# Logits, ranks, rows and lists of every batch moved to PSUM banks T and U; weight conversions due later, their stores issued from GpSimd

## The chip, the cores and the metric

The kernel runs on one core of a Trainium2 chip. The metric is the device time of one execution in microseconds (us); where several executions are timed, the median stands for them. A profiled execution gives the trace, with a time of its own.

## The reference

Three stages follow each other, with 4 batches of 448 tokens, 12 heads of 64 and a model width of 768:

```python
scores = cap * tanh(q @ k.T / sqrt(64) / cap)           # attention, per batch and head
attn = exp(scores - max); attn /= attn.sum + 1e-9
x = concat_heads(attn @ v)                               # 1792 x 768
h = x @ w_in; g = h * clip(h + 3, 0, 6) / 6              # FFN, d_ff = 2048
y = g @ w_out
logits = y @ w_gate; e = argmax(logits)                  # 8 experts, one per token
out = softmax(logits)[e] * sigmoid(y @ w_output_gate)[e] * (relu(y @ w1[e]) @ w2[e])
```

The FFN's weights `w_in` and `w_out` arrive as 64-bit floats, all else as 32-bit floats.

## The kernel before

**Stages.** Attention is done per pair of heads (24 pairs, 6 per batch). For a pair, TensorE transposes q and k, which ScalarE (L495) and VectorE (L499) split into a high and a low part (`qk`); TensorE forms the scores (L527) in the double banks S0 and S1; ScalarE takes tanh (L536) and exp (L540); VectorE sums the exponentials (`es`, L548); TensorE multiplies with v (L558) and sums over rows (L564); the division follows (L591 to L601), and the result stands in `xTa` or `xTb` in two parts. The FFN of a batch has 28 products (16 with a slice of `w_in`, 12 with one of `w_out`), each of three passes (L610 to L612). A product's weights come from DRAM into `wr` (L633, on SP's queue) and are split into `ws` by ScalarE (L636) and VectorE (L639). After a batch's FFN come the routing (`route`: logits L762, their transposes L773, ranks L799 and L800), the token rows (`rows`: transposes L854, eight groups per batch, copied out at L291 or L293) and a listing of tokens (`listing`, L899). After the last batch the experts' slots follow (`ring`, `hTm`, L1423).

**Conversion of the FFN's weights.** `cv` converts the 64-bit weights to 32 bits once, in 56 parts, two per product of the first batch's FFN. A part is loaded on GpSimd's queue (L394) into one of five buffers, scaled by VectorE or ScalarE (L400, L402), put together by three VectorE operations (L405, L408, L411) in one of three `cva` tiles, and stored to DRAM (L416) on SP's queue, whence L633 loads it in each batch.

**Banks.** PSUM has the double banks S0 and S1 and the single ones T, U, F0 and F1. The FFN's products use F0 and F1 in turn. From the second batch on attention uses T (transposes of q and k, row sums) and U (product with v). Routing, rows and listing of batches 0, 1 and 3 take F0 and F1, those of batch 2 take T and U (`TU`).

**Order.** The program is issued by a planner (`Work.run`): each operation has a due time `at`, a length `ns`, what it comes after and the buffers it holds. For each engine the planner takes, of the operations that are ready in its own count of time, the one due first, and issues it. What comes out is a fixed order per engine; on the chip each engine works its list off in that order and waits on semaphores. `conv` parts were due at `i * 4.4e3` for the first 16 (the attention of batch 0 is planned from 0 to `T0` = 70e3) and 30e3 ahead of their product for the others:

```python
at = i * 4.4e3 if i < 16 else max(T0, t_ff(i // 2) - 30e3)
x = work.add("pool", at - 6e3, 1500, load, ...)
stored[i] = work.add("sp", at + 3e3, 500, store, [y], [ha], size=w * 512)
```

Of the kernel before, what the change touches and what calls it, by code (L numbers as in the profile page):

```python
# [68 lines left out]
class Work:  # L69
# [5 lines left out]
    LAG = {"pe": 200, "act": 150, "dve": 130, "pool": 150, "sp": 0}  # L75
    TO_PE = {"act": 160, "dve": 70}
    WINDOW = 10240 / 3
    PRE, POST, RATE = 1400, (1100, 2000), 0.36

    def __init__(self):  # L80
        self.ops = []
# [12 lines left out]
    def run(self):  # L94
# [10 lines left out]
        soon = {e: [] for e in self.LAG}  # L105
        due = {e: [] for e in self.LAG}
        free = dict.fromkeys(self.LAG, 0)
        tick = cols = 0
        line = 0
        slow = 2  # L110
# [13 lines left out]
        while done < len(self.ops):  # L124
# [23 lines left out]
            if e == "pe":  # L148

                x = t  # L150
# [31 lines left out]
def attention_ffn_moe(  # L182
# [15 lines left out]
    nc = tc.nc  # L198
    B, H, S, D = q.shape
# [113 lines left out]
    Sp, Tp, Up, F, U2 = banks("S0", "S1"), banks("T"), banks("U"), banks("F0", "F1"), banks("U", "F1")  # L313
# [25 lines left out]
    work = Work()  # L339
# [3 lines left out]
    T0, T1, TL = 70e3, 174e3, 120e3  # L343
# [14 lines left out]
    def t_ff(i):  # L358
        b, j = divmod(min(i, B * NW - 1), NW)
        if i >= B * NW:  # L360
            return T0 + (B - 1) * T1 + TL + (i - B * NW) * 3e3
        x = cost[j] / cost[-1]
        return T0 + b * T1 + x * (T1 if b < B - 1 else TL)
# [7 lines left out]
    wv_out = w_out_i.rearrange("(t p) (d w) -> p t d w", p=128, w=256)  # L371
    stored, turned_w = {}, {}

    def cv(i):
        key, j = parts[i][:-1], parts[i][-1]
        at = i * 4.4e3 if i < 16 else max(T0, t_ff(i // 2) - 30e3)
        h, ha = F64.take(), CVA.take()
        if key[0] == "i":
            n = KD // 2
            src = wv_in[:, j * n:(j + 1) * n, key[1], :]  # L380
            dst = ws_in[key[1]]
        else:
            n = NH2
            o = key[1] * HF + j * n
            src = wv_out[:, o:o + n, key[2], :]
            dst = ws_out[key[1]][key[2]]
        t = h.t[:, 0:n]
        w = n * 128
        lo = t.rearrange("p t w two -> p (t w) two")[:, :, 0]
        g = t.rearrange("p t w two -> p (t w) two")[:, :, 1]  # L390
        a = ha.t[:, 0:w]

        def load():
            G.dma_start(out=t.rearrange("p t w two -> p t (w two)"), in_=src)  # L394

        def scaled(eng):

            t = g.bitcast(F32)
            if eng == "dve":
                V.tensor_scalar(out=t, in0=t, scalar1=2.0 ** -112, scalar2=None, op0=ALU.mult)  # L400
            else:
                A.activation(out=t, in_=t, func=ACTF.Copy, scale=2.0 ** -112)  # L402

        def b0():
            V.tensor_scalar(out=a, in0=lo, scalar1=29, scalar2=None, op0=ALU.logical_shift_right)  # L405

        def b1():
            V.scalar_tensor_tensor(out=a, in0=g, scalar=3, in1=a, op0=ALU.logical_shift_left, op1=ALU.bitwise_or)  # L408

        def b2():  # L410
            V.scalar_tensor_tensor(  # L411
                out=a, in0=g, scalar=-(1 << 31), in1=a, op0=ALU.bitwise_and, op1=ALU.bitwise_or
            )

        def store():
            nc.sync.dma_start(  # L416
                out=dst[:, j * n:(j + 1) * n], in_=a.rearrange("p (t w) -> p t w", w=128).bitcast(F32)
            )

        x = work.add("pool", at - 6e3, 1500, load, [turned_w.get(i - 3)] if i < 16 else [], [h], size=w * 1180)  # L420
        s = work.add(("dve", "act"), at, (65 + w // 2, 30 + w), scaled, [x], [h])
        y = work.add("dve", at, 65 + w // 2, b0, [x], [h, ha])
        y = work.add("dve", at, 65 + w, b1, [s, y], [h, ha])
        y = turned_w[i] = work.add("dve", at, 65 + w, b2, [y], [h, ha])
        stored[i] = work.add("sp", at + 3e3, 500, store, [y], [ha], size=w * 512)


    NH = B * H
# [321 lines left out]
    def route(b):  # L750

        t0 = t_ff((b + 1) * NW) + 1e3
        soon = t0 + SOON if b == B - 1 else t0 + 2e3
        R = TU if b == B - 2 else F
        hl, hr = R.take(), ROUTE.take()
        ys = [yT[b, d] for d in range(KD)]
        lp = hl.t
# [84 lines left out]
    def rows(b, c, ys, hr, wd):  # L842
# [3 lines left out]
            rowbuf[b] = ROWS.take(), []  # L846
        hw, done = rowbuf[b]
        for half in range(2):
            hp = (TU if b == B - 2 else F).take()

            def trans(half=half, tp=hp.t):
                for j in range(KD // 2):
                    d = half * (KD // 2) + j
                    nc.tensor.transpose(tp[:P, j * 128:(j + 1) * 128], ys[d][0].t[:, c * P:(c + 1) * P], ident)  # L854

            o = c * RW + half * w_rows
            src = hp.t[:P, 0:w_rows]
            x = work.add("pe", t0, 330, trans, [y[1] for y in ys], [hp] + [y[0] for y in ys])
            x = work.add(
                ("act", "dve"), t0 + 1e3, (371, 465), copier(hw.t[:, o:o + w_rows], src), [x], [hp, hw])  # L860
            done.append(x)
# [13 lines left out]
    def listing(b):  # L875
# [6 lines left out]
        for j, h in enumerate((h0, h1)):  # L882
# [8 lines left out]
        done.append(work.add(  # L891
            "dve", t0, 535, lambda: V.tensor_tensor(
                out=m, in0=m, in1=ids.to_broadcast([P, C, PG]), op=ALU.mult), [x], [h2, hr]))
        hp = (TU if b == B - 2 else F).take()
        acc = hp.t[:PG, 0:128]

        def sums():
# [270 lines left out]

    plan = [(t_head(2 * n - 2) - 1 if n else -2, lambda n=n: pair_qk(n)) for n in range(NH // 2)]
    plan += [(t_head(2 * n) if n else -1, lambda n=n: pair(n)) for n in range(NH // 2)]  # L1170
    plan += [(i * 4.4e3 if i < 16 else t_ff(i // 2) - 30e3, lambda i=i: cv(i)) for i in range(len(parts))]
    plan += [(t_ff(i), lambda i=i: step(i)) for i in range(len(ff))]
    plan += [(t_ff(5) + 1, quiet), (t_ff(NW) - 1, zeros)]
    fin = {}
# [377 lines left out]
```

## Time and profile before

| | |
|---|---|
| three runs | 1067.36 us median (1066.06 to 1068.58) |
| the profiled execution | 1065.96 us, span 1064.2 us |
| busy: TensorE, VectorE, ScalarE, GpSimd | 96%, 68%, 62%, 9% of the span |
| DMA | 199.24 MB, 187 GB/s over the span |

The first 85 us are batch 0's attention, with conversions between; then FFN products and the attention of the next batch run side by side until about 600 us, the last FFN until 740 us, and the experts' slots until the end. A busy TensorE is one whose matmuls overlap or follow without a gap; VectorE's and ScalarE's shares are means over stages that differ.

### The profile page before, as it was taken

What the parts mean: (1) busy time and instruction counts of PE and PEld (TensorE: products, weight loads), DVE (VectorE), ACT (ScalarE), POOL (GpSimd) and SP (SyncE); (2) the same over time, 40 slices, a digit from 0 to 9 for tenths busy, and PEclk for the clock granted to TensorE, in tenths of its full rate; (3) what the DMA queues carried; (4) which work ended last, traced back from release to release, by engine and by line L of the source; (5) the groups of instructions that cost most, each with busy time, mean ns of one, the idle gap of its engine ahead of it and who ended that gap; (6) DMA issues with size and microseconds to landing.
All of it is one profiled execution on the core that took longest, in us unless ns stands there. A gap on an engine that the chain in (4) does not pass through costs nothing.

```text
span 1064.2 us, 17020 instructions
## 1 busy us (share of the span) xinstructions
PE 1024.5 (96%) x5764; PEld 799.7 (75%) x5764; DVE 725.5 (68%) x1154; ACT 661.0 (62%) x917; POOL 93.6 (9%) x122
## 2 busy tenths in 40 slices
PE   6879999999999999999999999999899999999996
PEld 4436778876778787678878799998787777887774
DVE  5999988975763664674475482535986767786763
ACT  6987767755654764474575262535576776876763
POOL 3211222110000000000000100000030101111001
PEclk9989999999999999999999999999899999999999
DMA  9789889962242333234222266354358789979464
GB/s 277 234 244 270 260 289 282 292 206 84 69 157 83 100 125 91 84 103 144 83 86 87 64 247 217 122 189 165 112 164 304 260 289 335 316 260 339 142 187 126
DMA packets 113998, 199.24 MB, mean 187 GB/s; under 512 B 43579, under 2 KB 68027, under 8 KB 113345
## 3 DMA queue, kind: packets, MB, share of 16 engines
q1 hardware_dynamic: 104304, 161.90, 47.0%
q0 software_dynamic: 9600, 36.19, 10.6%
q8 instruction: 47, 0.77, 0.3%
q14 instruction: 47, 0.38, 0.1%
HBM read 224.19 MB, written 25.76 MB: 235 GB/s over the span
## 4 chain that ended last, share of the span: by engine, by line
PE 70%; DVE 14%; issue 10%; DMA 3%; ACT 2%; POOL 0%; SPq 0%; POOLq 0%; DVEq 0%; ACTq 0%
PE F L610 12%; PE F L612 11%; PE F L611 11%; PE S L610 6%; PE S L611 6%; PE S L612 6%; PE U L558 5%; PE S L527 5%; PE F L1423 2%; DVE es L548 2%; DMA out_dram<-y,tkd 2%; DVE cva L408 1%; DVE cva L411 1%; DVE ring L1274 1%; DVE ws L639 1%
## 5 line engine op out<-in xcount | busy, mean ns | idle before, releaser
L639 DVE TENSOR_TENSOR ws<-wr,ws 128x768 fp32r<-128x768 f32 (+1 forms) x112 | 119.4, 1067 | 79.5 <-ACT ws L636 76.9
L636 ACT ACTIVATE ws<-wr 128x768 fp32r<-128x768 f32 (+1 forms) x112 | 104.6, 934 | 38.8 <-PE F L611 27.1
L610 PE MATMUL F<-gT,ws 128*128 128x448 f32 x320 | 120.1, 375 | 1.6 <-ACT xTb L293 1.0
L611 PE MATMUL F<-gT,ws 128*128 128x448 f32 x320 | 117.0, 366 | 0.0
L612 PE MATMUL F<-gT,ws 128*128 128x448 f32 x320 | 117.0, 366 | 0.0
L536 ACT ACTIVATE S<-S,rcap 112x896 f32<-112x896 f32 x96 | 91.1, 980 | 20.0 <-PE S L527 19.4
L540 ACT ACTIVATE ee<-S,capt 112x896 f32<-112x896 f32 x96 | 93.5, 1015 | 0.2
L527 PE MATMUL S<-qk 64*112 64x448 f32 x576 | 77.3, 393 | 12.2 <-ACT qk L495 5.2
L610 PE MATMUL S<-ring,hTm 128*128 128x384 f32 x224 | 81.9, 366 | 0.0
L527 PEld LDWEIGHTS S<-qk 64*112 64x112 f32 x576 | 47.5, 176 | 40.8 <-issue 12.7
L611 PE MATMUL S<-ring,hTm 128*128 128x384 f32 x224 | 76.4, 341 | 0.9 <-DVE ring L1274 0.9
L612 PE MATMUL S<-ring,hTm 128*128 128x384 f32 x224 | 76.3, 341 | 0.0
L610 PE MATMUL F<-xTa,ws 128*128 128x448 f32 x192 | 73.7, 384 | 0.8 <-DVE lg L780 0.6
L610 PE MATMUL F<-xTb,ws 128*128 128x448 f32 x192 | 73.6, 383 | 0.9 <-DVE lg L780 0.6
L610 PEld LDWEIGHTS F<-gT,ws 128*128 128x128 f32 x320 | 60.1, 188 | 16.0 <-issue 8.7
L1274 DVE TENSOR_TENSOR ring<-w2B,ring 128x768 fp32r<-128x768 f32 x56 | 52.6, 955 | 28.5 <-ACT ring L1270 26.9
L612 PE MATMUL F<-xTb,ws 128*128 128x448 f32 x192 | 70.2, 366 | 0.0
L611 PE MATMUL F<-xTb,ws 128*128 128x448 f32 x192 | 70.2, 366 | 0.0
L558 PE MATMUL U<-ee,v 112*64 112x448 f32 x336 | 70.0, 556 | 0.0
L612 PE MATMUL F<-xTa,ws 128*128 128x448 f32 x192 | 69.8, 364 | 0.0
L611 PE MATMUL F<-xTa,ws 128*128 128x448 f32 x192 | 69.5, 362 | 0.0
L663 ACT ACTIVATE r<-F,three 128x448 f32<-128x448 f32 x64 | 40.6, 635 | 45.3 <-PE F L612 44.5
(291 smaller groups left out, 2263.8 us busy)
## 6 DMA issues: line engine op xcount, KB each, us to landing
wr<-wsi SPq DMA_DIRECT2D x64, 384.0 KB
wr<-wso SPq DMA_DIRECT2D x48, 512.0 KB
w1A<-in_moe_w_dram SPq DMA_DIRECT2D x42, 512.0 KB
w2A<-in_moe_w_dram SPq DMA_DIRECT2D x56, 384.0 KB
w1B<-in_moe_w_dram SPq DMA_DIRECT2D x42, 512.0 KB
w2B<-in_moe_w_dram SPq DMA_DIRECT2D x56, 384.0 KB
spare<-in_moe_w_dram SPq DMA_DIRECT2D x72, 256.0 KB
spare<-in_moe_w_dram SPq DMA_DIRECT2D x96, 192.0 KB
```

Of the source, the lines that this page charges most:

```text
L527: nc.tensor.matmul(out=h.t[:P, r, 0:S], lhsT=w[o, 1, i, (c0 + c) * P:(c0 + c + 1) * P], rhs=w[o, 0, j], start=(t == 0), stop=(t == 2))
L536: lambda sv=sv: A.activation(out=sv, in_=sv, func=ACTF.Tanh, scale=rcap[:P]), [s] + caps, [h])
L540: lambda sv=sv, he=he: A.activation(out=he.t, in_=sv, func=ACTF.Exp, scale=capt[:P]), [x], [h, he])
L548: lambda he=he, one=one: V.tensor_tensor(out=es, in0=one.t, in1=he.t, op=ALU.add),
L558: nc.tensor.matmul(out=uv[64 * r:64 * r + 64, 0:S], lhsT=by_head(hv)[:, r, c], rhs=et[c][0].t[:, r], start=(c == 0), stop=(c == C - 1))
L610: nc.tensor.matmul(out=acc, lhsT=lh, rhs=rh, start=first, stop=False)
L611: nc.tensor.matmul(out=acc, lhsT=lh, rhs=rl, start=False, stop=False)
L612: nc.tensor.matmul(out=acc, lhsT=ll, rhs=rh, start=False, stop=last)
L636: lambda: A.activation(out=s[:, 0, 0:n], in_=t, func=ACTF.Copy), [x], [hw, hs])
L639: lambda: V.tensor_tensor(out=s[:, 1, 0:n], in0=t, in1=s[:, 0, 0:n].bitcast(F32), op=ALU.subtract),
L663: "act", t1, 518, lambda: A.activation(out=r, in_=acc, func=ACTF.Relu, bias=three), [last], [ha, hr])
L1274: lambda: V.tensor_tensor(out=hs.t[:, 1, 0:w], in0=raw(), in1=hs.t[:, 0, 0:w].bitcast(F32), op=ALU.subtract),
```

## The change

The conversions' due times are set anew: the first 16 are due from `T0 - 16e3` on at steps of 1e3, the others 40e3 ahead of their product. Their stores go from SP's queue to GpSimd's, with the same due time as the load. Batches 0 and 1 use T and U for routing, rows and listing, as batch 2 did (batch 3 keeps F0 and F1). Three of the planner's own numbers change: GpSimd is taken to be free from 2800 ns on, its DMAs to need 4000 instead of 2000 ns after the transfer, and a load's issue to take 800 instead of 1500 ns.

```diff
-    PRE, POST, RATE = 1400, (1100, 2000), 0.36
+    FIRST = 2800
+    PRE, POST, RATE = 1400, (1100, 4000), 0.36
...
+        free["pool"] = self.FIRST
...
+    def conv_at(i):
+        return T0 - 16e3 + i * 1e3 if i < 16 else max(T0, t_ff(i // 2) - 40e3)
+
     def cv(i):
-        at = i * 4.4e3 if i < 16 else max(T0, t_ff(i // 2) - 30e3)
+        at = conv_at(i)
...
         def store():
-            nc.sync.dma_start(
+            G.dma_start(
...
-        x = work.add("pool", at - 6e3, 1500, load, [turned_w.get(i - 3)] if i < 16 else [], [h], size=w * 1180)
+        x = work.add("pool", at - 6e3, 800, load, [turned_w.get(i - 3)] if i < 16 else [], [h], size=w * 1180)
...
-        stored[i] = work.add("sp", at + 3e3, 500, store, [y], [ha], size=w * 512)
+        stored[i] = work.add("pool", at - 6e3, 800, store, [y], [ha], size=w * 512)
...
-        R = TU if b == B - 2 else F
+        R = TU if b <= B - 2 else F
...
-            hp = (TU if b == B - 2 else F).take()
+            hp = (TU if b <= B - 2 else F).take()
...
-        hp = (TU if b == B - 2 else F).take()
+        hp = (TU if b <= B - 2 else F).take()
...
-    plan += [(i * 4.4e3 if i < 16 else t_ff(i // 2) - 30e3, lambda i=i: cv(i)) for i in range(len(parts))]
+    plan += [(conv_at(i), lambda i=i: cv(i)) for i in range(len(parts))]
```

The planner's new order shows at three places. Lines of the changed kernel stand 5 higher than before from `cv` on.

ScalarE's list begins, before (L402 scales a conversion's part, `f_161` and `f_162` are load buffers):

```order
L402 ACTIVATE f_161<-f_161 128x384
L495 ACTIVATE qk_147<-T 128x448
L495 ACTIVATE qk_147<-F_139 128x448
L402 ACTIVATE f_162<-f_162 128x384
L536 ACTIVATE S_135<-S_135,rcap 112x2x448
L540 ACTIVATE ee_149<-S_135,capt 112x896
```

and now (L500 is the old L495, L541 the old L536, L545 the old L540, L407 the old L402):

```order
L500 ACTIVATE qk_147<-T 128x448
L500 ACTIVATE qk_147<-F_139 128x448
L500 ACTIVATE qk_148<-T 128x448
L541 ACTIVATE S_135<-S_135,rcap 112x2x448
L545 ACTIVATE ee_149<-S_135,capt 112x896
L541 ACTIVATE S_136<-S_136,rcap 112x2x448
L500 ACTIVATE qk_148<-F_139 128x448
L545 ACTIVATE ee_150<-S_136,capt 112x896
L541 ACTIVATE S_135<-S_135,rcap 112x2x448
L407 ACTIVATE f_162<-f_162 128x384
```

The splits of q and k, tanh and exp now stand ahead of the first scaling, which stood at the head of the list.

GpSimd's list after its constants, before:

```order
L394 DMA f_161<-in_moe_w_in_dram 128x3x256
L394 DMA f_162<-in_moe_w_in_dram 128x3x256
L394 DMA spare<-in_moe_w_in_dram 128x3x256 x3
L394 DMA f_161<-in_moe_w_in_dram 128x3x256
L394 DMA f_162<-in_moe_w_in_dram 128x3x256
```

and now (L399 loads a part, L421 stores one, `wsi_65` being its place in DRAM):

```order
L399 DMA f_161<-in_moe_w_in_dram 128x3x256
L399 DMA f_162<-in_moe_w_in_dram 128x3x256
L399 DMA spare<-in_moe_w_in_dram 128x3x256
L421 DMA wsi_65<-cva_163 128x384
L399 DMA spare<-in_moe_w_in_dram 128x3x256
L421 DMA wsi_65<-cva_164 128x384
L399 DMA spare<-in_moe_w_in_dram 128x3x256
L421 DMA wsi_66<-cva_165 128x384
```

Each load from the fourth on stands behind the store of an earlier part: three loads are ahead of a store for the first 12 parts, five from the fourteenth on. SP's list has lost its 56 stores.

TensorE's list at batch 0's routing, before (L773 transposes the logits, L489 a pair's q or k, L799 and L800 are the ranks):

```order
L489 MATMUL T<-ident,q_142 128x112 x4
L773 MATMUL F_139<-ident,spare 112x128 x4
L489 MATMUL T<-ident,k_144 128x112 x4
L610 MATMUL F_139<-xTb_172,ws_182 128x448
L611 MATMUL F_139<-xTb_172,ws_182 128x448
L612 MATMUL F_139<-xTb_172,ws_182 128x448
L610 MATMUL F_139<-xTb_173,ws_182 128x448
L611 MATMUL F_139<-xTb_173,ws_182 128x448
L612 MATMUL F_139<-xTb_173,ws_182 128x448
L799 MATMUL F_140<-oh,ones 128x32
```

and now (L778 is the old L773, L859 the old L854, L615 to L617 the old L610 to L612):

```order
L532 MATMUL S_135<-qk_148 112x448 x6
L532 MATMUL S_136<-qk_148 112x448 x6
L778 MATMUL U<-ident,spare 112x128 x4
L615 MATMUL F_140<-xTb_174,ws_181 128x448
L616 MATMUL F_140<-xTb_174,ws_181 128x448
L617 MATMUL F_140<-xTb_174,ws_181 128x448
L615 MATMUL F_140<-xTb_175,ws_181 128x448
L616 MATMUL F_140<-xTb_175,ws_181 128x448
L617 MATMUL F_140<-xTb_175,ws_181 128x448
L859 MATMUL U<-ident,spare 112x128 x3
```

The logits' transposes leave F_139, which the FFN's next product takes, for U, and the product that follows goes on in the bank it had.

## Rows read from the trace of the kernel before

**Rows 1.** The page, part 1: busy time, share and instructions of TensorE and VectorE.

```profile
PE 1024.5 (96%) x5764; PEld 799.7 (75%) x5764; DVE 725.5 (68%) x1154; ACT 661.0 (62%) x917; POOL 93.6 (9%) x122
```

**Rows 2.** Busy time by stretch: stretch, length, then us and instructions per engine.

```profile
core 0: us, PE busy (x) PEld busy (x) DVE busy (x) ACT busy (x) POOL busy (x), PEclk, DMA share, GB/s
0.00:20.00 20.00, 11.62 (x94) 8.19 (x96) 8.93 (x20) 9.40 (x13) 8.36 (x25) 1.00 0.88 265
20.00:80.42 60.42, 50.79 (x366) 24.38 (x364) 57.36 (x106) 55.73 (x76) 11.56 (x15) 0.92 0.86 247
85.50:220.20 134.70, 134.33 (x725) 105.88 (x724) 126.24 (x224) 100.44 (x147) 26.15 (x33) 1.00 0.89 278
256.00:310.00 54.00, 51.26 (x299) 37.49 (x296) 39.63 (x81) 36.66 (x56) 0.00 (x0) 1.00 0.37 112
430.00:482.00 52.00, 49.73 (x293) 36.19 (x292) 38.22 (x80) 35.23 (x51) 0.00 (x0) 1.00 0.31 90
482.00:740.00 258.00, 257.39 (x1342) 219.86 (x1340) 134.60 (x225) 122.62 (x178) 6.37 (x19) 1.00 0.42 144
740.00:830.00 90.00, 84.37 (x455) 67.32 (x454) 72.76 (x127) 59.86 (x82) 12.91 (x8) 0.96 0.57 192
```

**Rows 3.** Timeline of TensorE up to the first FFN product: start, length, operation.

```profile
78.05 1.01 PE L489 MATMUL T<-ident,k 112*128 112x112 f32 x4 [1.89 <-DVE qk L499]
...
85.53 0.47 PE L610 MATMUL F<-xTa,ws 128*128 128x448 f32 x1
```

**Rows 4.** Timeline of VectorE: batch 0's eighteenth sum, the last conversion, its product's split.

```profile
79.34 1.08 DVE L548 TENSOR_TENSOR es<-es,ee 112x896 f32<-112x896 f32 x1
...
219.49 0.65 DVE L411 SCALAR_TENSOR_TENSOR cva<-f,cva 128x512 int32<-128x512 int32 x1
...
234.70 1.22 DVE L639 TENSOR_TENSOR ws<-wr,ws 128x1024 fp32r<-128x1024 f32 x1
```

**Rows 5.** VectorE's groups by form, 0 to 235 us: count, busy us, mean ns.

```profile
L408 DVE SCALAR_TENSOR_TENSOR cva<-spare,cva 128x384 int32<-128x384 int32 x19 | 10.3, 552 | 0.3
...
L408 DVE SCALAR_TENSOR_TENSOR cva<-spare,cva 128x512 int32<-128x512 int32 x14 | 9.4, 676 | 0.0
...
L405 DVE TENSOR_SCALAR cva<-spare 128x384 int32<-128x384 int32 x19 | 6.4, 351 | 3.1 <-DMA wsi<-cva 3.1
...
L400 DVE TENSOR_SCALAR spare<-spare 128x384 f32<-128x384 f32 x6 | 2.1, 353 | 0.0
...
L291 DVE CAST xTa<-ux 128x448 fp32r<-128x448 f32 x3 | 1.2, 388 | 0.0
```

**Rows 6.** Timeline at the start: the weight load, the first scaling, split, scores and tanh.

```profile
9.89 0.56 ACT L402 ACTIVATE f<-f 128x384 f32<-128x384 f32 x1 [7.79 <-DMA f<-in_moe_w_in_dram]
10.35 0.52 ACT L495 ACTIVATE qk<-T 128x448 fp32r<-128x448 f32 x1
...
11.35 0.71 PE L527 MATMUL S<-qk 64*112 64x448 f32 x2 [4.12 <-ACT qk L495]
...
13.64 0.98 ACT L536 ACTIVATE S<-S,rcap 112x896 f32<-112x896 f32 x1 [1.49 <-PE S L527]
```

**Rows 7.** Waits of TensorE, 255 to 330 us (batch 0's routing): us, times, longest.

```profile
PE F L773 <- DVE r L666: 1.4, 1, 1.4
PE F L610 <- DVE lg L780: 0.6, 1, 0.6
PE F L799 <- DVE oh L789: 0.3, 1, 0.3
PE F L610 <- DVE spare L291: 0.3, 1, 0.3
```

**Rows 8.** Busy time by stretch at batch 2's routing, which already uses T and U.

```profile
600.00:640.00 40.00, 40.00 (x220) 35.29 (x219) 30.51 (x80) 21.67 (x35) 0.00 (x0) 1.00 0.57 201
```

**Rows 9.** Line L394, the weight loads: issue in ns (min/median/max), then issue to landing.

```profile
L394 POOL DMA_DIRECT2D spare<-in_moe_w_in_dram x19: 743/758/767, 4.6 to 159.3; - x19
...
L394 POOL DMA_DIRECT2D f<-in_moe_w_in_dram x13: 741/758/1013, 2.8 to 150.7; - x13
...
DMA to landing us min/median/max: 4.2/6.0/10.1
```

## Prediction

> **What bounds the kernel now.** I read four views in turn. The page gives TensorE as busy for 96% of the span [rows 1], so little is to be had but in the stretches where it is not. The table by stretch shows these [rows 2]. From 85.5 to 220.2 us TensorE is busy for 134.33 of 134.70 us, from 482 to 740 for 257.39 of 258.00. It is short of work in four places: up to 80.42 us (11.62 of 20.00, then 50.79 of 60.42), at the routing of batches 0 and 1 (2.74 and 2.27 us idle in the rows from 256 and from 430), and from 740 to 830 (5.63 us). The change reaches the first three. In the first, VectorE is the full one: 57.36 of 60.42 us from 20 us on, while it idles for 11.07 of the first 20. TensorE's timeline ends that stretch with a wait for VectorE's split of a pair's k at 78.05, and then runs without a gap to the first FFN product at 85.53 [rows 3]. So the FFN starts when VectorE has worked off what its list holds ahead of the last attention steps of batch 0, of which I take the eighteenth sum, at 79.34 [rows 4], as the mark. TensorE's list holds the same number of score, transpose and v instructions ahead of the first FFN product in both kernels, so what it does from there on is not longer than before, and a start so much earlier ends so much earlier, if nothing starves it.
>
> **Term A, the attention of batch 0.** By the two orders, VectorE's list holds 18 conversions ahead of the eighteenth sum before, and 14 now, all of 384 columns (two of the 18 had 512); 7 scalings before, 9 now; 2 casts of `ux` before, 4 now; sums, splits, transposes and `ws` are the same in number. A conversion of 384 columns costs L405 + L408 + L411 = 0.351 + 0.552 + 0.552, the last taken at its twin's length [rows 5]: 1.455 us, four of them 5.82. The two wide ones cost 2 x (0.676 - 0.552) = 0.25 each more, at least: 0.5 together. Against that stand two scalings (2 x 0.353 = 0.71) and two casts (2 x 0.388 = 0.78). So VectorE has 5.82 + 0.5 - 0.71 - 0.78 = 4.8 us less ahead of the mark. This counts in full only if its idle time up to there (11.07 + 3.06 = 14.1 us, [rows 2]) stays. Two things pull at it. ScalarE's first scaling waited 7.79 us for a weight load, and behind it, in the same list, stood the split on which the first scores waited 4.12 us [rows 6]; now the splits come first, so the first tanh, at 13.64, can come up to 4.1 us sooner. On the other side VectorE has fewer conversions to fill its gaps with, and from the fourth part on a load stands behind a store that waits for its conversion, with three parts in flight: one period is at most load, two issues and a conversion over three, (6.0 + 2 x 0.76 + 1.5) / 3 = 3.0 us at the median landing and 4.4 at the longest, 10.1 [rows 9], while 14 conversions in 80 us need one every 5.7. I take the idle time as unchanged, between 4.1 us less and 3.1 us more (twice what it was from 20 us on): A is -4.8 us, between -8.9 and -1.7.
>
> **What A pulls along.** Four conversions now lie behind the first product, where VectorE is busy for 126.24 of 134.70 us, so 8.5 us are free. By the orders its list holds, ahead of the last conversion, one sum, one split, one reciprocal with its transpose, five scalings, a cast and an FFN sum more than before: 1.08 for the sum [rows 4], 5 x 0.353 and 0.388 [rows 5], and four of half the sum's columns at about half its length, 2.2: 5.4 us. The last conversion ended at 220.14; the split of its product ran at 234.70, 14.6 us later [rows 4]. A store and a load lie between; at 6.0 each, the nearest row, they leave 2.6 us. If it ends 5.4 us later while TensorE comes 4.8 us earlier, 7.6 us are missing by then. But the 8.5 free us lie ahead of it, and the planner has put more attention and later products in TensorE's list there: I cost it at nothing, and keep the bound of all of A.
>
> SP loses 56 stores; the loads of q, k, v and `wr` behind them no longer wait for a conversion. GpSimd gains 56 issues, at 0.76 us each 42 us in a stretch of 220 where it is idle most of the time. I cost both at nothing: bytes and transfers stay the same.
>
> **Term B, the banks.** In batch 0's routing TensorE waited 1.4 us for bank F that an FFN product still held (L773), 0.6 for the logits' reduction to free it again (L610), and 0.3 for a row group's copy (L291); the 0.3 for the ranks' input (L799) is no bank's doing [rows 7]. Batch 1 lost 2.27 us in all [rows 2]. Of 2.74 + 2.27 = 5.0 I take off the 0.3 of the ranks twice: 4.4 us can go. What is late next: T and U, which the attention of the next batch uses. In the new order of batch 0 six FFN matmuls or a pair's scores stand between nearly any two uses of these banks by the routing. Batch 2 does all of this in T and U and TensorE is busy for 40.00 of 40.00 us [rows 8], though no attention runs then. I leave 0.9 us for waits of this kind: B is -3.5, between -5.0 and, all used up again, 0.
>
> **The rest.** Beyond 600 us the parts of some slots change their order among themselves; the instructions are the same. The stage from 740 to 830 has 5.63 us of idle TensorE that may shrink or grow; I take nothing, with some 2 us either way in the range.
>
> **The sum.** -4.8 - 3.5 = -8.3 us. The profiled execution took 1065.96 us, 1.40 below the median of the runs, 1067.36. Against it the sum gives 1057.7; against the median, which is what is measured, **1059.1 us**.
>
> **Rivals.**
> - *A is given back* (0.20). VectorE does the same work in all, and TensorE, ahead by 4.8 us, finds the weights of the first FFN's last third late. For it: 7.6 us missing by the reckoning above. Against it: 8.5 us free on VectorE. B stays: 1067.36 - 3.5 = 1063.9 us.
> - *The waits move to T and U* (0.12), and the kernel is slower. A batch's routing uses them 12 times (logits, their transposes, ranks, eight row groups, listing), two batches 24 times, and TensorE works its list in order, so a bank not yet copied out stops products and attention alike. From a mean wait of (4.8 + 4.4) / 24 = 0.38 us it eats the gain. At 0.6 us, the wait for the logits' reduction [rows 7], it costs 14.4: 1067.36 - 9.2 + 14.4 = 1072.6 us. Against it stands batch 2 [rows 8]; for it, that attention holds T and U for a whole product with v.
> - *Nothing is left* (0.10). The order is only a list; if VectorE waits for weight loads with three parts in flight, its idle time grows by the 4.8 us it saved, and small waits at T and U take B: 1067.4 us.
> - *GpSimd's issues become long* (0.02). All 112 issues fall into the first 220 us; at 220 / 112 = 1.96 us each GpSimd would be full. Of the 32 issues in the rows the median is 0.758 us and the longest 1.013 [rows 9], though VectorE was nearly always busy. At three times the longest, 3.04 us, they would take 340 us and the conversions end 120 us late, at some 1180 us in all. The Trainium skill's page "SBUF — State Buffer", section "Who interferes with whom", speaks for this rival and against the change: it says that a DMA issued from GpSimd can't get its descriptors written while VectorE runs a copy, cast or tensor_scalar in a two-port mode, and that one issued from SP doesn't suffer; elsewhere the same page gives 3100 ns for such a DMA that takes 620 alone. Here the 32 issues, with VectorE's casts and scalings beside them, are lengthened by 0.26 us at most, so the trace sides against it.
>
> **How the numbers follow.** The forecast has 0.56, the rivals 0.20, 0.12, 0.10 and 0.02. About 0.2% (2.1 us) is what a measurement of this kernel can tell from no change. Faster: 0.56 + 0.20 = 0.76; the same: 0.10; slower: 0.12 + 0.02 = 0.14. The low end is A and B at their best with 2 us from the last stage, 1067.36 - 8.9 - 5.0 - 2 = 1051.5, the high end the case in which nothing is left: 1067.5. What lies beyond is the slower cases and little else.
>
> **What would show it.** Right: the first FFN product (L615) starts near 81 us and not 85.5; the first tanh comes before 13.64; VectorE's eighteenth sum comes near 74.5; TensorE stays busy from there to 256 us; the waits L778 and L615 on a bank in the two routings are gone, and TensorE's idle time there falls from 5.0 to some 1.5 us. Wrong: waits of `cva` or of L407 on the weight loads in the first 80 us (A), TensorE waiting for `ws` between 190 and 250 us (A given back), waits of L778, L859, L494 or L563 on T or U (B).

## The result and the profile after

The changed kernel takes 1056.01 us, the median of 6 runs (1053.09 to 1057.96), against 1067.84 for the kernel before in its 6 runs (1066.06 to 1074.1): a ratio of 0.988, 95% interval 0.9852 to 0.9909. The forecast was 1059.1 us. The profiled execution of the changed kernel took 1053.09 us, the lowest of its runs, with a span of 1051.4; that of the kernel before had a span of 1064.2. So the two traces stand 12.8 us apart and the medians 11.8.

Lines from the conversion on have numbers 5 higher after the change (6 in experiments 5, 6 and 12, 7 in experiment 7, by the lines that these add): L615 is the old L610, L532 the old L527, L541 the old L536, L553 the old L548, L416 the old L411, L399 the old L394 and L421 the store that was L416.

The page of the changed kernel, part 1, answers to [rows 1]:

```profile
PE 1017.0 (97%) x5764; PEld 796.7 (76%) x5764; DVE 725.2 (69%) x1157; ACT 659.5 (63%) x914; POOL 124.9 (12%) x178
```

TensorE has the same 5764 matmuls and is busy for 7.5 us less: busy time counts a matmul at a lower clock as longer, so a part of the gain is hidden in it. The table by stretch of the changed kernel, beside [rows 2]; the stretch from 220.2 is new:

```profile
core 0: us, PE busy (x) PEld busy (x) DVE busy (x) ACT busy (x) POOL busy (x), PEclk, DMA share, GB/s
0.00:20.00 20.00, 13.83 (x118) 9.47 (x118) 9.19 (x20) 11.54 (x15) 6.22 (x23) 1.00 0.75 204
20.00:80.42 60.42, 51.88 (x382) 26.90 (x383) 58.79 (x113) 54.90 (x74) 21.20 (x32) 1.00 0.85 250
85.50:220.20 134.70, 133.84 (x715) 103.79 (x714) 128.91 (x230) 98.50 (x143) 47.44 (x73) 1.00 0.91 283
220.20:256.00 35.80, 35.80 (x192) 29.06 (x192) 22.37 (x31) 17.79 (x23) 3.13 (x2) 1.00 0.53 167
256.00:310.00 54.00, 54.00 (x309) 41.38 (x308) 35.71 (x76) 32.35 (x50) 0.00 (x0) 1.00 0.38 117
430.00:482.00 52.00, 52.00 (x302) 40.92 (x299) 34.48 (x73) 32.17 (x48) 0.00 (x0) 1.00 0.40 120
```

TensorE no longer idles at either routing (54.00 of 54.00, 52.00 of 52.00), and up to 80.42 us the clock column shows 1.00 where it showed 0.92. The same table for the kernel before, in the stretch that was not shown:

```profile
220.20:256.00 35.80, 34.80 (x188) 27.84 (x188) 19.23 (x28) 14.67 (x19) 1.00 (x1) 1.00 0.42 131
```

Marks in the two timelines tell where the 12.8 us arise. The first FFN product starts at 75.34 and not 85.53 (-10.2). By the attention's last division the lead is 16.7 us (575.1 against 591.8): the routings gave 5.0 and the stretch from 220 us on 1.0. By the last scatter of rows it is 18.2; the 2.0 us that these terms leave over are not taken apart here. And then 5.4 us of it go, after the last scatter, where no engine computes.

**Ahead of the FFN.** TensorE's timeline up to the first FFN product, changed kernel:

```profile
70.43 1.72 PE L563 MATMUL F<-ee,v 112*64 112x448 f32 x8
72.73 0.97 PE L569 MATMUL F<-es,ones 112*64 112x448 f32 x4 [0.58 <-DVE es L553]
73.64 1.48 PE L532 MATMUL S<-qk 64*112 64x448 f32 x12
75.34 0.47 PE L615 MATMUL F<-xTa,ws 128*128 128x448 f32 x1 [0.22 <-ACT us L596]
```

and the same four steps in the kernel before, between the lines of [rows 3]:

```profile
78.98 3.26 PE L558 MATMUL F<-ee,v 112*64 112x448 f32 x8
82.03 1.71 PE L564 MATMUL F<-es,ones 112*64 112x448 f32 x4
83.66 1.93 PE L527 MATMUL S<-qk 64*112 64x448 f32 x12
```

The same instructions took 3.26, 1.71 and 1.93 us and now take 1.72, 0.97 and 1.48. The table by stretch says why, first the kernel before, then the changed one:

```profile
75.00:78.00 3.00, 1.16 (x10) 0.59 (x8) 3.00 (x7) 3.00 (x6) 0.00 (x0) 0.97 0.79 224
78.00:86.00 8.00, 7.96 (x30) 3.70 (x31) 7.93 (x15) 4.23 (x7) 2.00 (x3) 0.58 1.03 268
```

```profile
70.00:76.00 6.00, 5.20 (x31) 2.57 (x32) 5.76 (x11) 3.44 (x7) 0.81 (x2) 1.00 1.06 346
```

The granted clock was 0.58 of full speed there, near the lower of its two levels (1.2 of 2.4 GHz), after TensorE had been busy for 1.16 of the 3 us from 75 to 78. Now it is 1.00.

VectorE's eighteenth sum, the mark of [rows 4], and the last conversion in the changed kernel's timeline:

```profile
71.59 1.09 DVE L553 TENSOR_TENSOR es<-es,ee 112x896 f32<-112x896 f32 x1
...
219.16 0.65 DVE L416 SCALAR_TENSOR_TENSOR cva<-f,cva 128x512 int32<-128x512 int32 x1
```

The mark is 7.75 us earlier. The table up to the mark, the kernel before and then the changed one, splits this:

```profile
0.00:79.34 79.34, 61.33 (x454) 32.33 (x456) 65.20 (x124) 64.22 (x87) 19.17 (x39) 0.95 0.86 252
```

```profile
0.00:71.59 71.59, 58.06 (x458) 31.15 (x460) 59.57 (x116) 60.15 (x78) 24.83 (x50) 1.00 0.79 230
```

VectorE works 5.63 us less up to the mark (65.20 to 59.57) and idles 2.12 less (14.14 to 12.02). Little of that lies at the start: 0.26 up to 20 us (11.07 to 10.81, by the first row of [rows 2] and of the table above) and 1.86 from there to the mark (3.07 to 1.21). The first tanh comes 2.4 us sooner than in [rows 6], but VectorE, which had conversions to do there before, now waits 4.5 us in all for ScalarE's splits up to 20 us:

```profile
11.24 0.98 ACT L541 ACTIVATE S<-S,rcap 112x896 f32<-112x896 f32 x1 [0.86 <-PE S L532]
```

```profile
DVE qk L504 <- ACT qk L500: 4.5, 3, 1.9
```

The last conversion begins at 219.16, against 219.49 before, and TensorE waits little in the stretch where the FFN's weights could have been late. Its waits from 90 to 215 us:

```profile
PE F L615 <- DVE r L671: 0.4, 2, 0.2
PE T L494 <- DVE qk L504: 0.2, 1, 0.2
PE F L617 <- DVE ws L644: 0.2, 1, 0.2
```

**The end.** After the last scatter GpSimd's queue steps a counter for each of three skipped slots and then drains. The kernel before, first its timeline, then the two lines' own views (count, ns min/median/max, first and last start):

```profile
1059.79 0.97 POOL L1135 DMA_INDIRECT out_dram<-y,tkd  x1 [2.58 <-DMA out_dram<-y,tkq]
```

```profile
L1511 POOLq INC_SWDGE_SEM  x3: 333/347/376, 1060.4 to 1061.7; - x3
...
L1548 POOLq DRAIN  x3: 46/103/1195, 1062.0 to 1064.0; - x3
```

and the same two views of the changed kernel:

```profile
1041.56 0.97 POOL L1140 DMA_INDIRECT out_dram<-y,tkd  x1 [2.56 <-DMA out_dram<-y,tkq]
```

```profile
L1516 POOLq INC_SWDGE_SEM  x3: 1180/1193/1207, 1042.2 to 1045.1; - x3
...
L1553 POOLq DRAIN  x3: 46/103/4233, 1046.3 to 1051.1; - x3
```

From the last scatter to the end of the span it took 1064.2 - 1059.79 = 4.4 us; now it takes 9.8. Three counter steps of 1.193 in place of 0.347 are 2.5 us, and the longest drain, 4.233 in place of 1.195, is 3.0.

**GpSimd's issues.** The lines of the loads and the stores in the changed kernel, beside [rows 9]:

```profile
L421 POOL DMA_DIRECT2D wsi<-cva x32: 557/575/895, 13.1 to 177.4; - x32
L421 POOL DMA_DIRECT2D wso<-cva x24: 540/557/692, 81.7 to 220.1; - x24
```

```profile
L399 POOL DMA_DIRECT2D spare<-in_moe_w_in_dram x19: 741/743/872, 4.6 to 160.9; - x19
```

No issue is long: a store takes 0.56 us, and the longest of all 112 issues took 0.999.

### The profile page after: what moved, and what is told of

The parts are those of the page before. It is cut to its first block, busy times and chain, and to the rows that moved or that the text cites. A ratio compares the mean times of both kernels' runs of the same rounds, so it can differ in the third digit from the quotient of the medians.

```text
span 1051.4 us, 17036 instructions
## 1 busy us (share of the span) xinstructions
PE 1017.0 (97%) x5764; PEld 796.7 (76%) x5764; DVE 725.2 (69%) x1157; ACT 659.5 (63%) x914; POOL 124.9 (12%) x178
## 4 chain that ended last, share of the span: by engine, by line
PE 70%; DVE 13%; issue 10%; DMA 4%; ACT 2%; POOL 0%; SPq 0%; POOLq 0%; DVEq 0%; ACTq 0%
PE F L615 12%; PE F L617 11%; PE F L616 11%; PE S L615 6%; PE S L616 6%; PE S L617 6%; PE U L563 5%; PE S L532 4%; PE F L1428 3%; DVE cva L413 2%; DMA out_dram<-y,tkd 2%; DVE cva L416 2%; DVE es L553 1%; DVE ws L644 1%; DVE ring L1279 1%
## 5 line engine op out<-in xcount | busy, mean ns | idle before, releaser
L615 PE MATMUL F<-gT,ws 128*128 128x448 f32 x320 | 120.9, 378 | 0.0
L617 PE MATMUL F<-gT,ws 128*128 128x448 f32 x320 | 117.1, 366 | 0.2 <-DVE ws L644 0.2
L541 ACT ACTIVATE S<-S,rcap 112x896 f32<-112x896 f32 x96 | 91.3, 977 | 13.2 <-PE S L532 12.7
L545 ACT ACTIVATE ee<-S,capt 112x896 f32<-112x896 f32 x96 | 93.6, 1012 | 0.3
L532 PE MATMUL S<-qk 64*112 64x448 f32 x576 | 75.2, 387 | 6.6 <-DVE qk L504 4.7
L615 PE MATMUL S<-ring,hTm 128*128 128x384 f32 x224 | 81.4, 363 | 0.0
L617 PE MATMUL S<-ring,hTm 128*128 128x384 f32 x224 | 76.1, 340 | 0.0
L615 PE MATMUL F<-xTa,ws 128*128 128x448 f32 x192 | 73.9, 385 | 1.0 <-DVE r L671 0.4
L615 PE MATMUL F<-xTb,ws 128*128 128x448 f32 x192 | 73.8, 384 | 0.0
L615 PEld LDWEIGHTS F<-gT,ws 128*128 128x128 f32 x320 | 60.1, 188 | 15.1 <-issue 10.8
L532 PEld LDWEIGHTS S<-qk 64*112 64x112 f32 x576 | 46.7, 174 | 31.5 <-issue 11.0
L617 PE MATMUL F<-xTb,ws 128*128 128x448 f32 x192 | 70.2, 366 | 0.0
L617 PE MATMUL F<-xTa,ws 128*128 128x448 f32 x192 | 69.8, 363 | 0.0
```

What stands on the lines that cost most here:

```text
L532: nc.tensor.matmul(out=h.t[:P, r, 0:S], lhsT=w[o, 1, i, (c0 + c) * P:(c0 + c + 1) * P], rhs=w[o, 0, j], start=(t == 0), stop=(t == 2))
L541: lambda sv=sv: A.activation(out=sv, in_=sv, func=ACTF.Tanh, scale=rcap[:P]), [s] + caps, [h])
L545: lambda sv=sv, he=he: A.activation(out=he.t, in_=sv, func=ACTF.Exp, scale=capt[:P]), [x], [h, he])
L615: nc.tensor.matmul(out=acc, lhsT=lh, rhs=rh, start=first, stop=False)
L617: nc.tensor.matmul(out=acc, lhsT=ll, rhs=rh, start=False, stop=last)
```

## The experiments

The theory after this reading: the conversions' due times give what is won ahead of the FFN, the banks give 5 us, and the stores on GpSimd cost 5.4 us at the end and bring nothing. Times of one group of runs stand against the kernel before in the same group, whose median lay between 1067.98 and 1070.27 us.

**1. The due times alone.** The changed kernel, with the planner's three new numbers, and these lines as before (with the two lines of `hp` below the one of `R`):

```diff
-            G.dma_start(
+            nc.sync.dma_start(
...
-        stored[i] = work.add("pool", at - 6e3, 800, store, ...)
+        stored[i] = work.add("sp", at + 3e3, 500, store, ...)
...
-        R = TU if b <= B - 2 else F
+        R = TU if b == B - 2 else F
```

> The kernel before with the conversions' new due times (and the planner's numbers that go with them); the stores stay on SP, the banks of batches 0 and 1 stay as they were. Theory (the gain ahead of the FFN comes from the conversions' times alone): first FFN product at 75 to 77 us against 85.5, the waits at the routings of batches 0 and 1 still there (some 5 us), the time from the last scatter to the end back at 4.4 us: about 1057 to 1059 us. Rival (SP's queue, rid of the stores, is what lets q, k and v come earlier): the first product comes at 80 us or later, about 1062 us.

Measured: 1060.01 us (6 runs) against 1067.98, ratio 0.9928 (0.9915 to 0.9941): 8.0 us. The eighteenth sum came at 72.77, 6.6 us ahead of the kernel before, but the first FFN product only at 79.88: TensorE's clock was at 0.71 from 70 to 75 us and at 0.61 from 75 to 80, and the tail from the mark to the product took 7.1 us in place of 3.75. The waits of the routings stayed (51.52 of 54.00 and 49.63 of 52.00 busy), and the end took 4.5 us. So the times carry the gain up to the mark, and the rival's start at 80 us has another cause than SP's queue: the clock. Of the lead of 5.7 us at the first product 2.5 are left by the attention's last division (589.3 against 591.8): TensorE idles for 2.9 us from 85.5 to 256, against 1.4 before. By the last scatter the lead is 6.2 (1053.62).

**2. The stores alone.** The changed kernel, with the planner's three new numbers, the banks as before and

```diff
-        return T0 - 16e3 + i * 1e3 if i < 16 else max(T0, t_ff(i // 2) - 40e3)
+        return i * 4.4e3 if i < 16 else max(T0, t_ff(i // 2) - 30e3)
```

> The changed kernel with the old due times and the old banks; only the stores' issue is on GpSimd. Theory (what is lost after the last scatter is the price of the stores' issues on GpSimd): the first FFN product stays at 85 us or comes up to 1 us later, the last scatter to the end takes 9.8 us in place of 4.4 us, so 1071 to 1074 us. Rival (the loss at the end belongs to the times or the banks): 4.4 us after the last scatter and about 1068 us.

Measured: 1067.49 us (12 runs), ratio 0.9987 (0.9975 to 0.9999). The end is as expected, 9.8 us after the last scatter with steps of 1193 ns and a drain of 4233, so it comes with the stores and not with times or banks. But the total was missed: the first product came at 82.4 and the last scatter at 1056.67, 3.1 us ahead of the kernel before. Here 15 conversions lay ahead of the mark and not 18. The mark is 1.4 us earlier (77.94), the other 1.7 lie in the tail behind it, 4.49 us in place of 6.19. The new order does bring something ahead of the end, and the end takes it back; how much of it belongs to the stores' queue and how much to the planner's numbers this run doesn't tell.

**3. The banks alone.** The kernel before with

```diff
-        R = TU if b == B - 2 else F
+        R = TU if b <= B - 2 else F
...
-            hp = (TU if b == B - 2 else F).take()
+            hp = (TU if b <= B - 2 else F).take()
...
-        hp = (TU if b == B - 2 else F).take()
+        hp = (TU if b <= B - 2 else F).take()
```

> The kernel before with the banks T and U for the logits, ranks, rows and lists of batches 0 and 1 as well, nothing else. Theory: TensorE has no idle time at either routing, 5 us less, 1062 to 1063 us, the first FFN product as before at 85.5 us and 4.4 us after the last scatter. Rival (the waits were covered by the clock or by later work): the waits go and 2 us or less of it reaches the end, 1066 us or more.

Measured: 1059.98 us (6 runs), ratio 0.9925 (0.9904 to 0.9946). TensorE is busy for all of both stretches, by the table:

```profile
256.00:310.00 54.00, 54.00 (x309) 41.08 (x309) 39.16 (x81) 34.68 (x53) 0.00 (x0) 1.00 0.38 108
430.00:482.00 52.00, 52.00 (x301) 39.43 (x300) 39.45 (x81) 34.28 (x52) 0.00 (x0) 1.00 0.37 106
```

The last scatter came 5.9 us earlier (1053.88) with the first product at 84.5. This looks like 1.0 ahead of the FFN and the 5.0 of the routings, but the trace shows other parts. The mark came 1.7 us later (81.03), and the product 1.0 earlier only because the tail took 3.45 us in place of 6.19, at the full clock. From 85.5 to 256 us TensorE idles for 5.3 us, against 1.4 before (the kernel before, then this one):

```profile
85.50:256.00 170.50, 169.13 (x912) 133.72 (x912) 145.47 (x251) 115.11 (x165) 27.14 (x33) 1.00 0.79 247
```

```profile
85.50:256.00 170.50, 165.24 (x884) 129.43 (x883) 146.52 (x253) 113.32 (x162) 27.95 (x34) 1.00 0.79 246
```

By the attention's last division the lead is 4.1 (587.7 against 591.8). The medians show 8.0 us with an interval of 5.8 to 10.3, and experiments 1 and 4, which differ in the banks alone, lie 7.3 us apart by theirs. So the banks' gain reaches the end and is more than the 5.0 us of idle time at the routings; what makes up the rest was not traced.

**4. All but the stores.** The changed kernel with the first two pairs of lines of experiment 1, the banks as changed.

> The changed kernel with the stores' issue back on SP, due times and banks as changed. Theory (the end costs 5.4 us for the stores on GpSimd and they bring nothing): the first FFN product at 75 to 76 us, no idle time at the routings, 4.4 us after the last scatter: 1050 to 1052 us, below the changed kernel. Rival (stores on SP hold up the loads behind them): the first product 3 us or more later and the time at 1054 us or more.

Measured: 1052.69 us (4 runs), ratio 0.9855 (0.9839 to 0.9871), below the changed kernel. Due times and banks add up: 8.0 and 8.0 alone, 15.3 together. The first product came at 80.89, at the lower clock again (0.56 from 75 to 80 us), which is the rival's sign; the time is not. The end, in the timeline and in the two lines' views:

```profile
1048.16 0.97 POOL L1140 DMA_INDIRECT out_dram<-y,tkd  x1 [3.43 <-DMA out_dram<-y,tkq]
```

```profile
L1516 POOLq INC_SWDGE_SEM  x3: 333/347/376, 1048.8 to 1050.0; - x3
...
L1553 POOLq DRAIN  x3: 46/103/1187, 1050.4 to 1052.3; - x3
```

4.4 us from the last scatter, as in the kernel before, to a few ns in each row.

**5. Half of the stores.** The changed kernel with

```diff
-            G.dma_start(
+            (G if i % 2 == 0 else nc.sync).dma_start(
...
-        stored[i] = work.add("pool", at - 6e3, 800, store, ...)
+        q = ("pool", at - 6e3, 800) if i % 2 == 0 else ("sp", at + 3e3, 500)
+        stored[i] = work.add(*q, store, ...)
```

> The changed kernel with every second store of a conversion (odd number) issued by SP, the 28 others by GpSimd. Theory (the time after the last scatter grows with the number of stores that GpSimd issued): half of the 5.4 us, so about 7.1 us after the last scatter, each counter step of a skipped slot about 0.77 us and the closing drain about 2.7 us; about 1054 us. Rival (a step: any store on GpSimd brings all of it, or none below some number): 9.8 or 4.4 us after the last scatter.

Measured: 1058.82 us against 1070.27, ratio 0.9897 (0.9875 to 0.9919). 7.8 us after the last scatter, steps of 834 ns, a drain of 2845: between the two ends as expected, if not in the middle. The time is no better than the changed kernel's: the eighteenth sum came at 76.20 and the first product at 82.82.

**6. The first 16 stores.** As experiment 5 with `i < 16` in place of `i % 2 == 0`.

> The changed kernel with only the first 16 conversions' stores on GpSimd, the 40 later ones on SP. Theory (SP's queue matters ahead of the FFN only, the end by the count): VectorE's 18th sum at 71.5 to 73 us as in the changed kernel, the first product 3.7 us later where the clock holds, and 16/56 of 5.4 us, so 6 us, after the last scatter: 1050 to 1052 us, below the version with all stores on SP (1052.7). Rival (what the move brings ahead of the FFN is the clock's chance and no saving): 1054 us or more.

Measured: 1055.10 us, ratio 0.9857 (0.9834 to 0.9879), as low as experiment 4's. The sum at 72.66, the product 3.46 us later at 76.12 with the clock at 1.00, and 6.7 us after the last scatter (steps of 747 ns, drain 2437).

**7. Twice the loads.** Experiment 4 with

```diff
-            G.dma_start(out=t.rearrange("p t w two -> p t (w two)"), in_=src)
+            tt = t.rearrange("p t w two -> p t (w two)")
+            G.dma_start(out=tt[:, 0:2], in_=src[:, 0:2])
+            G.dma_start(out=tt[:, 2:n], in_=src[:, 2:n])
...
-        x = work.add("pool", at - 6e3, 800, load, ...)
+        x = work.add("pool", at - 6e3, 1600, load, ...)
```

> The changed kernel with all stores on SP and each of the 56 conversions' loads cut into two DMAs, both on GpSimd: as many issues there as in the changed kernel, with the bytes of the kernel before. Theory (the end pays for the number of DMAs issued by GpSimd): 9.8 us after the last scatter and about 1058 us. Rival (it pays for bytes or packets, or for stores): 4.4 us after the last scatter and 1053 us.

Measured: 1067.14 us, ratio 0.9972 (0.9955 to 0.9989). The profiled execution was the slowest of its eight, 1071.18. The end is longer than either expected: 14.3 us after the last scatter, by the two lines' views:

```profile
L1518 POOLq INC_SWDGE_SEM  x3: 1760/1773/1786, 1055.8 to 1060.2; - x3
...
L1555 POOLq DRAIN  x3: 46/103/6602, 1062.0 to 1069.2; - x3
```

No store is on GpSimd here, and GpSimd's queue moved as many bytes as before the change (36.19 MB). So the end is not the stores' own, and not bytes. With as many DMAs as the changed kernel it cost 4.5 us more, so it is not their number alone. The last scatter itself came 7 us later than in experiment 4, 3.6 of them in one wait of TensorE for `ux` just after 80 us.

**8. Nearly all on SP.** Experiment 4 with

```diff
-            G.dma_start(out=t.rearrange("p t w two -> p t (w two)"), in_=src)
+            (G if i < 16 else nc.sync).dma_start(out=t.rearrange("p t w two -> p t (w two)"), in_=src)
...
-        x = work.add("pool", at - 6e3, 800, load, ...)
+        x = work.add(*(("pool", at - 6e3, 800) if i < 16 else ("sp", at - 6e3, 500)), load, ...)
```

> The changed kernel with all stores on SP, and the loads of the 40 later conversions on SP as well: GpSimd issues 16 of the conversions' DMAs, against 56 in the kernel before and 112 in the changed one. Theory (what the end costs falls with the DMAs that GpSimd issued, below the kernel before too): 2 to 3.5 us after the last scatter against 4.4, the closing drain under 1 us; 1050 to 1052 us against a before of 1068, if SP's queue carries the loads without being late. Rival (4.4 us is the floor): 4.4 us after the last scatter and no gain on the version with the stores alone on SP. Second rival (SP's loads wait for their buffers and hold up q, k, v and the weights behind them): 1055 us or more.

Measured: 1058.04 us against 1069.33, ratio 0.9895 (0.9871 to 0.9919). The theory fell. With only 16 of the conversions' DMAs on GpSimd the end is as long as in the changed kernel (timeline, then the two lines' views):

```profile
1047.03 0.97 POOL L1140 DMA_INDIRECT out_dram<-y,tkd  x1 [2.56 <-DMA out_dram<-y,tkq]
```

```profile
L1516 POOLq INC_SWDGE_SEM  x3: 1113/1127/1156, 1047.7 to 1050.8; - x3
...
L1553 POOLq DRAIN  x3: 46/103/3988, 1051.9 to 1056.5; - x3
```

The second rival gave the right time, but not by a late front: the first product came at 76.04. From there to the last scatter it takes 971.0 us, against 967.3 in experiment 4; whether SP's queue has a part in that was not traced.

**9. The other kind.** The changed kernel, stores on GpSimd, with the loads' edit of experiment 8.

> The changed kernel with the loads of the 40 later conversions on SP and all 56 stores on GpSimd: 72 of the conversions' DMAs on GpSimd, as many as in the version with the first 16 stores there (6.7 us after the last scatter, drain 2.44 us), but of the other kind. If the number decides whatever the kind: 6.7 us and 2.4 us again. If stores are what costs: nearer 9.8 us and 4.2 us. If loads are what costs: under 4.4 us.

Measured: 1052.16 us, ratio 0.9846 (0.9818 to 0.9874). 6.3 us after the last scatter, steps of 687 ns, a drain of 2192: near experiment 6, which has the same number, and not the same. The first product came at 80.36 though all stores are on GpSimd; the clock had fallen once more (0.76 from 70 to 76 us). So where the stores are issued does not decide that fall: experiment 8, with all of them on SP, had the clock at 1.00.

**10 and 11. The changed kernel and experiment 4 side by side.**

> The changed kernel again, beside the version with all stores on SP on one chip. Theory (the stores on GpSimd cost 5.4 us at the end and bring some 2 us ahead of the FFN): 3 us above that version. Rival (the difference came from two chips): within 1 us of it.

> The changed kernel with all stores on SP again, beside the changed kernel on one chip: 0.985 to 0.987 of the kernel before, against 0.988 to 0.989 for the changed one.

Measured: 1055.49 us (1052.54 to 1057.43, ratio 0.9872, 0.985 to 0.9893) and 1052.54 us (1051.25 to 1053.38, ratio 0.984, 0.9819 to 0.9861). The version with the stores on SP is 3.0 us below the changed kernel on the same chip, as theory 10 had it, though the two intervals touch. The changed kernel's trace shows the product at 76.63, the last scatter at 1043.44 and 9.9 us after it; the other's 82.81, 1047.20 and 4.5.

**12. The old number, other DMAs.** The changed kernel with the stores' edit of experiment 6 and the loads' edit of experiment 8, there with `i < 40`.

> The changed kernel with the first 16 stores on GpSimd and the 40 others on SP, and the loads of the last 16 conversions on SP: GpSimd issues 56 of the conversions' DMAs, as many as in the kernel before, but 16 of them are stores. If between 56 and 112 of them the end goes by their number: 4.4 us after the last scatter, drain near 1.2 us, and with the first FFN product at 76 us about 1049 to 1051 us, the lowest so far. If the end goes by which DMAs they are, or in what order: anything else, as the version with 16 loads alone on GpSimd had (9.7 us, drain 3.99 us), and 1054 to 1057 us.

Measured: 1055.36 us against 1068.32, ratio 0.9878 (0.9854 to 0.9901). 9.4 us after the last scatter, by the two lines' views:

```profile
L1517 POOLq INC_SWDGE_SEM  x3: 1113/1127/1156, 1044.7 to 1047.5; - x3
...
L1554 POOLq DRAIN  x3: 46/103/3988, 1048.7 to 1053.2; - x3
```

As many conversion DMAs on GpSimd as in the kernel before, and another end; 40 more than in experiment 8, and the same steps and drain to the nanosecond. The first product came at 75.88.

All ends together, by what GpSimd issued for the conversions (its 32 gathers and scatters come on top in each):

| loads, stores on GpSimd | kernels | counter step, ns | longest drain, ns | last scatter to end, us |
|---|---|---|---|---|
| 16, 0 | 8 | 1127 | 3988 | 9.7 |
| 56, 0 | before, 1, 3, 4, 11 | 347 | 1187 to 1207 | 4.4 to 4.5 |
| 40, 16 | 12 | 1127 | 3988 | 9.4 |
| 16, 56 | 9 | 687 | 2192 | 6.3 |
| 56, 16 | 6 | 747 | 2437 | 6.7 |
| 56, 28 | 5 | 834 | 2845 | 7.8 |
| 56, 56 | after, 2, 10 | 1193 | 4233 | 9.8 to 9.9 |
| 112 halves, 0 | 7 | 1773 | 6602 | 14.3 |

## Why the prediction was right, and where its sizes were off

**Term A** (forecast -4.8, bounds -8.9 to -1.7) came out at -7.75 us at the mark, inside its bounds, and at -10.2 at the first FFN product, beyond them. Its own step, fewer conversions ahead of the mark, held: 14 of them as the order had said, and 5.63 us less work. The step "I take the idle time as unchanged" was off by 2.12 us, and not for the reason that I had named for less idle time, the scores no longer behind a scaling. The first tanh did come sooner, at 11.24, but only 0.26 us of VectorE's idle time went up to 20 us; 1.86 went behind it, where I had allowed for more. The step that TensorE's tail is "not longer than before" was true and too cautious: it became 2.4 us shorter (6.19 to 3.75 from the mark to the product), since the clock did not fall: I had counted the tail's instructions and not the clock that they run at. That 0.92 in the clock column of [rows 2] was a cost that could have been priced, and I read past it. It is the least certain part of the gain: the tail took 3.45 to 3.75 us in experiments 3, 6, 7, 8, 10, 12 and the changed kernel, and 6.5 to 8.0 in 1, 4, 5, 9 and 11. The mark itself differs between two traces of one program by 1.6 us (71.59 in the changed kernel, 73.18 in experiment 10) and by 2.0 (74.31 in 4, 76.29 in 11). What makes the clock fall there stays open.

**What A pulls along** (forecast 0) is 0.8 us of waits from 90 to 215 us; the rival "A is given back" did not occur in the changed kernel, nor did "nothing is left". In experiment 1, where the routings kept their banks, a part of A went again by the last division. The 1.0 us of idle time from 220 to 256 us goes with the times too, and not with the banks: in that stretch TensorE is busy for 35.80 of 35.80 us in experiment 1 and for 33.81 in experiment 3, after 34.80 before.

**Term B** (forecast -3.5, bounds -5.0 to 0) came out at its best end in the changed kernel's trace, -5.0 at the routings. The 0.9 us that I held back for waits at T and U were not there; no wait of that rival's kind shows at either routing, and experiment 3 shows that the banks alone end the idle time. By the medians of experiment 3 the term is larger still, -8.0, beyond its bound.

**The stores on GpSimd**, "I cost both at nothing": this is the step that failed, in two ways that partly cancel. Ahead of the end the move brings something: about 2.4 us by the medians of 10 and 11 (5.4 at the end, 3.0 in the total). Where it arises is not shown: experiment 8, with all stores on SP, has the mark at 72.58, and the changed kernel in its two traces at 71.59 and 73.18. At the end it costs 5.4. I had counted the issues and looked at nothing that GpSimd's queue does after them. The rival of long issues named the right queue and the wrong place: the longest of the 112 issues took 0.999 us, beside a nearly full VectorE. By the rule of the Trainium skill's page "SBUF — State Buffer", section "Who interferes with whom", an issue can be held up while VectorE runs a cast or a scaling in a two-port mode. This trace shows no hold longer than one such instruction: the longest issues, 0.999 us of a load and 0.895 of a store, lie 0.25 and 0.32 above the medians of their rows (0.748 and 0.575), and a cast takes 0.388 [rows 5].

**The sum.** -7.75 at the mark and -2.4 from there to the product, -5.0 at the routings, -1.0 ahead of them, some -2.0 behind that is not taken apart, +5.4 at the end: -12.8, the difference of the two traces. The forecast of -8.3 was right in sign and in both mechanisms; it was too small by 3.5 us against the medians' 11.8, because the terms on top were larger than the end that I had missed. That the errors went against each other is luck: without the 5.4 us at the end, the median would be at 1050.6, below the range's low end of 1051.5.

**A better version.** Experiments 4 and 11 (1052.69 and 1052.54 us, stores back on SP) and 9 (1052.16, later loads on SP) lie 3 us below the changed kernel; by its ratio, 0.9857, experiment 6 belongs to them. Between them the intervals tell no difference. Experiment 9 has the last scatter at 1043.40 and still pays 6.3 us after it, so a version with that last scatter and the short end would save some 2 us more; none was found in these runs.

## What to carry to other kernels

Count the last microseconds too: this kernel, which issues DMAs from GpSimd, paid 4.4 to 14.3 us at its end in that queue's own instructions, where no engine's busy time shows it, and changes hundreds of microseconds earlier moved this by several us. The waits for a bank in the middle of a stage with a full TensorE were worth their whole length here, and more than the table of waits said (5.0 us of idle time, 7.3 to 8.0 by the medians). Where the clock column of a stretch is below 1.00, a change ahead of it can win or lose the clock's share as well (2.4 us here); price it as a term, with both ends. And one trace of a stretch with such a clock is one draw: compare two of the same program before a difference of 2 us is given a cause.

## What the runs showed of the hardware

The time that GpSimd's queue needs after the last scatter goes with the DMAs that the program issues there. Where kernels issue the same DMAs from GpSimd, the counter steps agree (347 ns in five traces, 1193 in three), and the longest drain within 20 ns. It doesn't grow with the number: 16 loads give 3988 ns, 56 give 1195, 112 halves give 6602. Nor with bytes (the first moved 17.31 MB on GpSimd's queue, the second and third 36.19), nor by kind. Between 56 and 112 DMAs that include all 56 loads it rises with each group of stores (347, 747, 834, 1193 ns), and experiments 8 and 12 land on the same 1127 and 3988 with 40 DMAs between them. In these two GpSimd's queue moved 4352 and 8448 packets, 4096 apart. That looks like a count that starts again somewhere on the way; this is a guess, the packets of the other kernels (9600 for 347 ns, 8320 for 687, 10496 for 1773) do not follow a simple order, and it stays open.

TensorE's clock differed at one place among versions that do nearly the same there: 1.00 in experiments 6, 8, 10 and 12 around 70 to 76 us, and 0.61 from 75 to 83 us in experiment 11, with TensorE busy for 7.55 of 8.00, by the table by stretch:

```profile
75.00:83.00 8.00, 7.55 (x29) 3.24 (x30) 5.63 (x12) 4.79 (x8) 2.24 (x3) 0.61 0.75 207
```

In experiments 1, 4, 5, 9 and 11, where it fell, TensorE was busy for 2.25 to 3.54 of the 5 us from 70 to 75; in 6, 7, 8, 10, 12 and the changed kernel, where it stayed, for 3.08 to 4.42. The two overlap, and these runs don't tell what decides.
